# One expert pair moved last and done in half, the exponential table loaded first, and constants taken off ScalarE's queue

## The chip, the cores and the metric

The kernel runs on one core of a Trainium2 chip. The metric is the device time of one execution in microseconds (us). It was taken three times on the chip, and one further execution was profiled.

## What is computed

Three layers run one after the other; only the last one's rows leave the chip.

```python
x = attention(q, k, v)            # 4 x 8 heads x 576 x 64; half the heads local, half strided by 32
x = x / rms(x) * rms_g            # 2304 rows of 512
x = (silu(x @ w_gate) * (x @ w_val)) @ w_out          # d_ff 1536
logits = x @ w_gate2 + modality_bias[modality_id]     # 8 experts
e_idx = argmax(logits); gate_w = softmax(logits)[e_idx]
for e in range(8):                # each row goes through one expert only
    h = relu(x[e_idx == e] @ w1[e])                   # 512 -> 1024
    out[e_idx == e] = gate_w * (h @ w2[e])            # 1024 -> 512
```

Computed with the reference's own inputs, 103, 403, 237, 255, 427, 442, 192 and 245 rows go to experts 0 to 7. Of the first 2048 rows these are 96, 367, 223, 224, 372, 377, 173 and 216.

## The kernel before

The work is split into stretches that a scheduler lays out engine by engine, except the last one, which is written out by hand (`tc.manual_schedule()`).

**Front.** Attention is cut into units (a part of a batch's heads each). A unit's `scores` puts matrix products into a bank of the accumulator memory, VectorE masks them (L202), ScalarE takes the exponential (L212), VectorE divides by the sum, TensorE transposes (L241), ScalarE copies (L243), TensorE multiplies by v (L252), ScalarE copies out (L261, L267). `fill` (L120) issues matmuls on a tile of ones that nobody reads: 40 ahead of all, and 10 ahead of each of the first twelve units' scores. Loads of q, k and v go over SyncE's queue; constants and the gate weights (`raw`, L440, 36 pieces of 512 KB) go over ScalarE's queue. A piece of `raw` is converted in three steps: `conv_a` on GpSimd (L446), `conv_b` on VectorE (L450), `conv_c` on ScalarE and VectorE (L457, L458). Loads share eight completion semaphores in turn, and a load waits until the load that had its semaphore last has landed.

**Chunks.** The rows go in 9 chunks of 256 through the gated layer: `gate_val` (L505 to L507), `gelu_post` (L513 to L519), `ff_out` (L530 to L532). Each product of two 32-bit numbers is three matmuls on parts h and l. `slot()` places the remaining attention and conversions between; `at(s, f)` hangs a function on slot s. Chunks 0 and 1 are interleaved. Each chunk's rows are routed (`route_t` to `route_i`) and written to memory (`rows_d`).

**Experts.** An expert's rows are cut into pairs of two blocks of 128. `first_tables` (L861 on) sorts the experts when 2048 rows are routed: the one with most rows first, and the others in cyclic order behind it; it gives SyncE the first expert's number (`mi`, L869), and SyncE loads its weights (`stg`, L872). `tables` orders the pairs. The program has a fixed part for `BASE = 11` pairs; more pairs than that run under two `tc.If`, at the end. For a pair, `gather` picks row numbers on VectorE and fetches rows by an indirect load on GpSimd's queue (L982), `x_transpose` turns them (L1010) and splits them (L1014, L1015), `mm1` (L1032 to L1034) makes 96 matmuls of 256 columns, `relu_split` (L1042, L1043) the hidden layer, `mm2` (L1056 to L1058) 48 matmuls of 512 columns, and `finish` scales and writes rows by an indirect store (L1072). `split` (L998, L999) makes the next expert's weights into h and l. The last of the fixed pairs does `mm2` block by block, so that the first block's `finish` lies beside the second block's matmuls.

Of the kernel before, what the change touches and what calls it, by code (L numbers as in the profile page):

```python
# [10 lines left out]
F32 = mybir.dt.float32  # L11
# [15 lines left out]
CH = 256  # L27
# [21 lines left out]
def moe_kernel(  # L49
# [72 lines left out]
    n_fill = [0]  # L122

# [45 lines left out]
    def attention(u, banks):  # L169
# [7 lines left out]
        def scores():  # L177
# [5 lines left out]
            if n_fill[0] < 12:  # L183
                n_fill[0] += 1
                fill(sps[:, 384:], 10)
# [507 lines left out]
    tri32 = tmp_p.tile([128, 128], F32, tag="tmp", name="tri32")  # L693
# [4 lines left out]
    A.dma_start(out=wg_sb, in_=w_gate)  # L698
    mb = const.tile([128, 2, E], F32, name="mb")
    A.dma_start(out=mb, in_=mbias.unsqueeze(0).to_broadcast([128, 2, E]))  # L700
    md = const.tile([128, NT, 2], I32, name="md")
    A.dma_start(out=md, in_=modal.bitcast(I32).rearrange("p (t w) -> p t w", w=2))
    mf = tmp_p.tile([128, NT, 2], F32, tag="tmp", name="mf")
    V.tensor_copy(mf[:, :, 1], md[:, :, 0])
    V.tensor_scalar(out=mf[:, :, 0], in0=mf[:, :, 1], scalar1=-1.0, scalar2=1.0, op0=ALU.mult, op1=ALU.add)
    V.memset(carry, 0.0)
    V.memset(ids, 0.0)
    bt = tmp_p.tile([128, NT, E], F32, tag="tmp", name="bt")
    for m, dst in ((0, bsel), (1, bt)):
        V.tensor_tensor(  # L710
            out=dst,
            in0=mf[:, :, m].unsqueeze(2).to_broadcast([128, NT, E]),
            in1=mb[:, m].unsqueeze(1).to_broadcast([128, NT, E]),
            op=ALU.mult,
        )
    V.tensor_tensor(out=bsel, in0=bsel, in1=bt, op=ALU.add)
# [17 lines left out]
    fill(bank("mx")[:, :128], 40)  # L734
# [55 lines left out]

    DELAY = 2
# [36 lines left out]
    def late_open():  # L828
# [15 lines left out]
        tile_([128, E], "e_l")  # L844
        tile_([128, E, E], "lt")
# [13 lines left out]
        tile_([128, 1], "cnt", I32)  # L859
        tile_([128, 1], "cf")  # L860

    def first_tables():
# [14 lines left out]
        V.tensor_scalar(out=key, in0=iota8, scalar1=mf, scalar2=8.0, op0=ALU.is_lt, op1=ALU.mult)  # L877
# [50 lines left out]
    def tables2():  # L928
# [15 lines left out]
        yield  # L944
        V.tensor_copy(lt["cnt"], lt["cf"])
        yield

    def expert_part(e, i):
        return ew[ds(e, 1), i].rearrange("e p c -> (e p) c")

# [344 lines left out]
```

## Time and profile before

| what | us |
| --- | --- |
| median of three executions (lowest, highest) | 865.37 (864.83, 865.46) |
| the profiled execution, own time | 867.22 |
| its span from first to last instruction | 865.4 |
| TensorE busy in the span | 843.9 |
| VectorE busy | 508.9 |
| ScalarE busy | 381.5 |

The profiled execution took 1.85 us longer than the median run; its span lies 1.8 us below its own time. PE is TensorE's matmuls, PEld its weight loads, DVE VectorE, ACT ScalarE, POOL GpSimd, SP SyncE; a q behind a name is that engine's queue of instructions. Busy shares are averages over stretches with different limits, and a busy PE is not PE at its peak.

### The profile page before, as it was taken

To read this page: it belongs to the slowest core of one execution; us is meant where nothing else is said; L and a number is where in the kernel's file an instruction comes from. 1 tells how busy PE (TensorE), PEld (TensorE's weight loads), DVE (VectorE), ACT (ScalarE), POOL (GpSimd) and SP (SyncE) were. 2 spreads that over 40 slices of the span, in tenths; PEclk is the share of its full clock that TensorE was granted. 3 is DMA by queue.
4 is the path that set the end of the run, shared out by engine and by line. 5 is a ranking of instruction groups with operands and counts; after the bars stand their busy time and mean duration, and the time that the engine had idled before them with its cause. 6 is when DMAs were issued, how large, how long until landed. Compare 5 with 4: busy or idle time off the path is not lost.

```text
span 865.4 us, 18024 instructions
## 1 busy us (share of the span) xinstructions
PE 843.9 (98%) x6872; PEld 763.8 (88%) x6872; DVE 508.9 (59%) x1614; ACT 381.5 (44%) x935; POOL 85.7 (10%) x87
## 2 busy tenths in 40 slices
PE   8799999999999999999999999999999999999995
PEld 7688989998988998999999999998899999999994
DVE  4979984544653553644534536356877666666650
ACT  4756564344453254442332222234554554545440
POOL 1314410000000000000000000001131111111100
PEclk9879999999999999999999999999999999999998
DMA  8959211011111111200000000042396734675000
GB/s 247 355 174 348 93 33 47 19 51 41 47 50 34 38 48 54 54 21 26 6 5 26 1 25 2 2 166 79 105 347 207 226 111 130 227 221 166 25 25 22
DMA packets 33015, 84.46 MB, mean 98 GB/s; under 512 B 5122, under 2 KB 12850, under 8 KB 32920
## 3 DMA queue, kind: packets, MB, share of 16 engines
q1 hardware_dynamic: 23064, 54.50, 19.8%
q10 hardware_dynamic: 6336, 19.26, 6.1%
q0 software_dynamic: 3520, 9.45, 3.2%
q8 instruction: 58, 0.95, 0.5%
q14 instruction: 37, 0.30, 0.1%
HBM read 91.57 MB, written 10.49 MB: 118 GB/s over the span
## 4 chain that ended last, share of the span: by engine, by line
PE 76%; issue 11%; DVE 7%; DMA 3%; ACT 1%; POOL 1%; ACTq 0%; POOLq 0%; DVEq 0%; SPq 0%
PE gv L505 11%; PE gv L506 11%; PE gv L507 10%; PE o L530 5%; PE o L531 5%; PE o L532 5%; PE o L1056 3%; PE o L1058 3%; PE o L1057 3%; PE mx L252 2%; PE s L1032 2%; DVE wf L458 2%; PE s L1033 2%; PE s L1034 2%; PE gv L1032 2%
## 5 line engine op out<-in xcount | busy, mean ns | idle before, releaser
L505 PE MATMUL gv<-xh,wf 128*128 128x256 f32 x864 | 247.1, 287 | 2.4 <-DVE t L515 1.4
L506 PE MATMUL gv<-xl,wf 128*128 128x256 f32 x864 | 245.8, 285 | 0.1
L507 PE MATMUL gv<-xh,wf 128*128 128x256 f32 x864 | 245.8, 285 | 0.0
L505 PEld LDWEIGHTS gv<-xh,wf 128*128 128x128 f32 x864 | 163.5, 190 | 9.6 <-DVE t L515 3.2
L506 PEld LDWEIGHTS gv<-xl,wf 128*128 128x128 f32 x864 | 163.7, 189 | 4.9 <-issue 0.6
L507 PEld LDWEIGHTS gv<-xh,wf 128*128 128x128 f32 x864 | 163.9, 190 | 0.8 <-issue 0.2
L999 DVE TENSOR_TENSOR l<-stg,h 128x1024 fp32r<-128x1024 f32 x88 | 107.1, 1223 | 38.0 <-ACT h L998 37.8
L998 ACT CAST h<-stg 128x1024 fp32r<-128x1024 f32 x88 | 91.6, 1048 | 35.3 <-PE o L1058 25.9
L514 DVE SCALAR_TENSOR_TENSOR t<-t,gv 128x256 f32<-128x256 f32 x108 | 45.0, 417 | 92.0 <-ACT t L513 91.2
L513 ACT ACTIVATE t<-gv 128x256 f32<-128x256 f32 x108 | 41.2, 382 | 124.5 <-PE gv L507 114.5
L518 ACT CAST hh<-t 128x256 fp32r<-128x256 f32 x108 | 43.8, 405 | 79.9 <-DVE t L515 34.8
L530 PE MATMUL o<-wf,hh 128*128 128x512 f32 x192 | 77.0, 401 | 0.0
L531 PE MATMUL o<-wf,hh 128*128 128x512 f32 x192 | 76.1, 396 | 0.0
L532 PE MATMUL o<-wf,hl 128*128 128x512 f32 x192 | 75.0, 397 | 0.0
L1056 PE MATMUL o<-h,hT 128*128 128x512 f32 x176 | 70.6, 401 | 0.0
L1058 PE MATMUL o<-h,hT 128*128 128x512 f32 x176 | 68.8, 391 | 0.0
L1057 PE MATMUL o<-l,hT 128*128 128x512 f32 x176 | 68.5, 389 | 0.0
L519 DVE TENSOR_TENSOR hl<-t,hh 128x256 fp32r<-128x256 f32 x108 | 47.1, 436 | 35.9 <-ACT hh L518 35.5
L212 ACT ACTIVATE pr<-pr,mx 128x54 f32<-128x54 f32 (+1 forms) x160 | 52.4, 348 | 12.5 <-DVE mx L202 12.3
L982 POOL DMA_INDIRECT xg<-rows_d,gi x22 | 24.3, 1104 | 303.1 <-DMA stg<-in 142.8
L1032 PE MATMUL s<-xh,h 128*128 128x256 f32 x176 | 49.7, 282 | 0.0
L1033 PE MATMUL s<-xl,h 128*128 128x256 f32 x176 | 49.5, 281 | 0.0
(212 smaller groups left out, 1552.6 us busy)
## 6 DMA issues: line engine op xcount, KB each, us to landing
stg<-in SPq DMA_DIRECT2D x96, 512.0 KB
raw<-in ACTq DMA_DIRECT2D x36, 511.8 KB
rows_d<-x SPq DMA_DIRECT2D x18, 256.5 KB
qk<-in SPq DMA_DIRECT2D x14, 221.0 KB
qk<-in SPq DMA_DIRECT2D x8, 272.0 KB
qk<-in SPq DMA_DIRECT2D x8, 208.0 KB
v<-in SPq DMA_DIRECT2D x14, 108.0 KB
qk<-in SPq DMA_DIRECT2D x7, 167.0 KB
```

The source lines that it names most:

```text
L505: T.matmul(dst, wh[:, ks], xh[k], start=(k == order[0]), stop=False)
L506: T.matmul(dst, wh[:, ks], xl[k], start=False, stop=False)
L507: T.matmul(dst, wl[:, ks], xh[k], start=False, stop=(k == order[3]))
L530: T.matmul(o, h[:, ms], wh, start=(f == 0), stop=False)
L531: T.matmul(o, h[:, ms], wl, start=False, stop=False)
L532: T.matmul(o, l[:, ms], wh, start=False, stop=(f == NF - 1))
L998: A.copy(h, lt["stg", i])
L999: V.tensor_tensor(out=l, in0=lt["stg", i], in1=h.bitcast(F32), op=ALU.subtract)
L1032: T.matmul(dst, w[0][:, k, cs_], xh, start=(k == 0), stop=False)
L1056: T.matmul(ys[t][m], hh, w[0][:, c], start=(q == 0 and c == 0), stop=False)
L1057: T.matmul(ys[t][m], hh, w[1][:, c], start=False, stop=False)
L1058: T.matmul(ys[t][m], hl, w[0][:, c], start=False, stop=(q == 3 and c == 1))
```

## The change

Three things are edited. (1) `first_tables` looks for experts whose number of blocks is odd (estimated from the first 2048 rows), puts the last-numbered of them at the end of the order, and the eleventh pair runs through a new function `half_pair`, for its first block alone. Its second block, and the pairs past eleven, stand under a new `tc.If`. (2) The exponential's table load stands at ScalarE's start, in front of an exponential of an unread tile. Five loads (`tri32`, `iota`, `wg_sb`, `mb`, `md`) go from ScalarE's queue to GpSimd's, and what VectorE makes of them stands at slot 40. (3) `fill` makes 24 matmuls first instead of 40, and none ahead of the first unit.

```diff
-            if n_fill[0] < 12:
-                n_fill[0] += 1
+            if 0 < u < 12:
                 fill(sps[:, 384:], 10)
...
+    warm = sm.tile([128, 4], F32, tag="mx", name="warm")
+    V.memset(warm, 0.0)
...
+    A.activation(out=warm, in_=warm, func=AF.Exp)
...
-    A.dma_start(out=tri32, in_=cst3[:, 5])
-    V.tensor_copy(tri, tri32)
-    A.dma_start(out=iota, in_=iot)
...
-    fill(bank("mx")[:, :128], 40)
+    fill(bank("mx")[:, :128], 24)
...
+    def routing_constants():
+        tri32 = tmp_p.tile([128, 128], F32, tag="tmp", name="tri32")
+        G.dma_start(out=tri32, in_=cst3[:, 5])
+        V.tensor_copy(tri, tri32)
+        G.dma_start(out=iota, in_=iot)
+        G.dma_start(out=wg_sb, in_=w_gate)
...
+    at(40, routing_constants)
...
+        V.tensor_scalar(out=lt["ti"], in0=carry, scalar1=NCH / (NCH - 1.0), scalar2=127.0, op0=ALU.mult, op1=ALU.add)
...
+        V.tensor_reduce(out=hi, in_=od, op=ALU.max, axis=AX.X)
...
-                x_transpose(t + 1, s - 4)
+                x_transpose(t + 1, s - 4, (0,) if t + 2 == BASE else (0, 1))
...
+    def half_pair(t, m):
+
+        rs = slice(128 * m, 128 * m + 128)
+        rl = {}
+
+        def first(q):
+            p = bank(("s0", "s1", "gv", "gv")[q], 2 if q > 1 else 1)[:, :CH]
+            w = [a.rearrange("p (k f) -> p k f", k=4) for a in ws[q]]
+            for k in range(4):
+                xh, xl = (a[:, k % 2, rs] for a in xT[t, k // 2])
+                T.matmul(p, xh, w[0][:, k], start=(k == 0), stop=False)
+                T.matmul(p, xl, w[0][:, k], start=False, stop=False)
+                T.matmul(p, xh, w[1][:, k], start=False, stop=(k == 3))
+            r = rl[q] = sl_p.tile([128, CH], F32, tag="t", name="rl")
+            A.activation(out=r, in_=p, func=AF.Relu)
+
+        def turn(q):
+            pt = bank(("pt", "mx")[q % 2])[:, :CH]
+            r = rl.pop(q)
+            for c in range(2):
+                T.transpose(pt[:, c * 128:c * 128 + 128], r[:, c * 128:c * 128 + 128], ident)
...
+            A.copy(h, pt)
+            V.tensor_tensor(out=l, in0=pt, in1=h.bitcast(F32), op=ALU.subtract)
+
+        def second(q):
+            y = ys[t][m]
+            w = [a.rearrange("p (c d) -> p c d", c=2) for a in ws[4 + q]]
+            for c in range(2):
+                hh, hl = (hT[q][:, i, c * 128:c * 128 + 128] for i in range(2))
+                T.matmul(y, hh, w[0][:, c], start=(q == 0 and c == 0), stop=False)
+                T.matmul(y, hh, w[1][:, c], start=False, stop=False)
+                T.matmul(y, hl, w[0][:, c], start=False, stop=(q == 3 and c == 1))
+
+        ys[t] = {m: bank(f"o{m}")}
+        first(0)
+        first(1)
+        turn(0)
+        first(2)
+        turn(1)
+        first(3)
+        turn(2)
+        second(0)
+        turn(3)
+        for q in (1, 2, 3):
+            second(q)
+        finish(t, (m,), True)
...
+            if t == BASE - 1:
+                half_pair(t, 0)
+                return
...
+        left = nc.values_load(lt["more"][0:1, 0:1], min_val=0, max_val=N + NP2)
+        with tc.If(left > 0):
...
+            with tc.If(second > 0):
+                for q in range(2):
+                    x_transpose(BASE - 1, q, (1,))
+                half_pair(BASE - 1, 1)
```

The start of ScalarE's order before: eight loads of constants stand ahead of the table load and the first eleven exponentials (`pr`), and the first weight piece (`raw`) behind these.

```order
1 L691 DMA cs<-in 128x256
2 L692 DMA cs<-in 128x128
3 L694 DMA tri_128<-in 128x128
4 L696 DMA iota<-in 128x161
5 L697 DMA g_sb<-in 128x4
6 L698 DMA wg_sb<-in 128x32
7 L700 DMA mb<-in 128x16
8 L702 DMA md<-in 128x36
9 L212 ACT_TABLE_LOAD
10 L212 ACTIVATE pr<-pr,mx 128x54 x11
11 L440 DMA raw<-in 128x2047
```

The same place with the change.

```order
1 L692 DMA cs<-in 128x256
2 L681 ACT_TABLE_LOAD
3 L681 ACTIVATE warm<-warm 128x4
4 L693 DMA cs<-in 128x128
5 L694 DMA g_sb<-in 128x4
6 L209 ACTIVATE pr<-pr,mx 128x54 x11
7 L437 DMA raw<-in 128x2047
8 L240 COPY ptS<-o_256 54x512
9 L209 ACTIVATE pr<-pr,mx 128x54 x2
10 L240 COPY ptS<-pt 54x512
11 L209 ACTIVATE pr<-pr,mx 128x54 x2
12 L437 DMA raw<-in 128x2047
```

The table load now stands behind one load, and two loads are left between it and the exponentials. The second `raw` load stands one copy later than before; in the built program it takes the semaphore of an early load of v, where before it took that of the first `raw` load. The third `raw` load now waits for the first.

The start of GpSimd's order with the change; before, the 36 conversions (`CAST top<-raw`) followed the memset without anything between.

```order
6 L679 MEMSET top 128x1024
7 L775 DMA iota<-in 128x161
8 L776 DMA wg_sb<-in 128x32
9 L778 DMA mb<-in 128x16
10 L780 DMA md<-in 128x36
11 L443 CAST top<-raw 128x512 x14
12 L773 DMA tri_1892<-in 128x128
13 L443 CAST top<-raw 128x512 x22
```

Four loads come ahead of the first conversion, and the load of `tri` between the 14th and the 15th. VectorE's conversion of `tri` stands, with the change, in front of a `conv_b` (`raw<-raw,top`) behind the four maskings of a unit that before began at 73.23 us.

VectorE's order in `first_tables` with the change, from the maximum over the experts' counts (`carry`) to the number that SyncE waits for (`mi`); `ti` and `od` are new.

```order
1256 L872 TENSOR_REDUCE m<-carry 128x1
1257 L886 TENSOR_SCALAR ti<-carry 128x8
1258 L631 TENSOR_TENSOR rw<-rw,oh 128x16
1259 L873 TENSOR_SCALAR key<-carry,m 128x8
1260 L887 TENSOR_SCALAR ti<-ti 128x8
1261 L636 TENSOR_REDUCE sc<-rw 128x4
1262 L874 TENSOR_TENSOR key<-key,iota 128x8
1263 L890 CAST od<-ti 128x8
1264 L516 TENSOR_TENSOR hl<-t,hh 128x256
1267 L891 SCALAR_TENSOR_TENSOR od<-iota,od 128x8
1268 L642 TENSOR_SCALAR si<-si 128x2
1269 L876 TENSOR_SCALAR mi<-m 128x1
```

Four new instructions stand ahead of `mi`; six more stand behind it.

## Rows read from the trace of the kernel before

**Rows 1.** The page: busy us, share of the span and instructions of each engine.

```profile
PE 843.9 (98%) x6872; PEld 763.8 (88%) x6872; DVE 508.9 (59%) x1614; ACT 381.5 (44%) x935; POOL 85.7 (10%) x87
```

**Rows 2.** Four stretches: length, busy us of PE, PEld, DVE, ACT, POOL, clock, DMA.

```profile
0.00:18.00 18.00, 15.25 (x229) 13.21 (x229) 6.70 (x60) 5.91 (x19) 1.90 (x6) 1.00 0.83 230
18.00:49.00 31.00, 24.02 (x314) 19.03 (x314) 27.22 (x113) 22.74 (x63) 8.00 (x10) 0.74 0.80 296
49.00:116.00 67.00, 65.73 (x570) 59.45 (x570) 63.42 (x181) 40.40 (x124) 25.09 (x26) 0.97 0.56 199
...
597.00:856.00 259.00, 259.00 (x1705) 235.19 (x1703) 164.37 (x258) 123.84 (x160) 45.59 (x41) 1.00 0.46 151
```

**Rows 3.** Timeline, TensorE about the last pair and a transpose of rows.

```profile
778.01 0.60 PE L1010 MATMUL pt<-cs,xg 128*128 128x128 f32 x4
778.37 0.47 PE L1056 MATMUL o<-h,hT 128*128 128x512 f32 x1
...
833.58 0.28 PE L1032 MATMUL s<-xh,h 128*128 128x256 f32 x1
833.70 0.28 PE L1033 MATMUL s<-xl,h 128*128 128x256 f32 x1
...
855.43 0.39 PE L1057 MATMUL o<-l,hT 128*128 128x512 f32 x1
855.66 0.39 PE L1058 MATMUL o<-h,hT 128*128 128x512 f32 x1
```

**Rows 4.** Timeline, ScalarE's and VectorE's share of a pair, and the end.

```profile
836.63 0.60 ACT L1042 ACTIVATE hT<-s 128x512 fp32r<-128x512 f32 x1 [1.21 <-PE s L1034]
837.26 0.69 DVE L1043 SCALAR_TENSOR_TENSOR hT<-s,hT 128x512 fp32r<-128x512 f32 x1 [0.52 <-ACT hT L1042]
...
857.64 0.98 POOL L1072 DMA_INDIRECT out<-y,gi  x1 [4.49 <-ACT y L1067]
```

**Rows 5.** DMA issues of GpSimd: count, median us from issue to landing.

```profile
xg<-rows_d,gi POOLq DMA_INDIRECT x22, 3.5
out<-y,gi POOLq DMA_INDIRECT x22, 4.8
```

**Rows 6.** Timeline of the first 18 us: warm-up, table load, first weight pieces.

```profile
1.06 5.05 PEld L120 LDWEIGHTS <-ones 128*128 128x128 bf16 x50 [1.06 <-DVE ones L682]
6.22 0.67 PE L191 MATMUL s<-qk 64*64 64x54 f32 x16
6.82 0.56 PEld L120 LDWEIGHTS <-ones 128*128 128x128 bf16 x10
6.88 1.28 ACT L212 ACT_TABLE_LOAD   x1 [6.88 <-DMA g_sb<-in]
9.89 0.36 ACTq L440 DMA_DIRECT2D raw<-in  x1
17.53 0.53 ACT L267 COPY xs<-mx 128x216 f32<-128x216 f32 x1 [3.58 <-DMA raw<-in]
18.05 0.69 DVE L450 SCALAR_TENSOR_TENSOR raw<-raw,top 128x512 int32<-128x512 int32 x1 [3.69 <-POOL top L446]
21.17 0.76 POOL L446 CAST top<-raw 128x512 f16<-128x512 bf16 x1 [3.15 <-DMA raw<-in]
48.84 0.80 PE L505 MATMUL gv<-xh,wf 128*128 128x256 f32 x2 [0.73 <-ACT xh L410]
```

**Rows 7.** Timeline about the first pair's rows: the expert's number, the gather, TensorE's wait.

```profile
573.33 0.15 DVE L869 TENSOR_SCALAR mi<-m 128x1 int32<-128x1 f32 x1
...
594.46 0.55 PE L1010 MATMUL pt<-cs,xg 128*128 128x128 f32 x3 [0.34 <-DMA xg<-rows_d,gi]
```

**Rows 8.** Timeline: VectorE's work on constants before, GpSimd's conversions, an indirect load's issue.

```profile
10.50 0.30 DVE L710 TENSOR_TENSOR bsel<-mf,mb 128x144 f32<-128x144 f32 x1
...
70.33 2.10 POOL L446 CAST top<-raw 128x512 f16<-128x512 bf16 x2 [2.48 <-DMA raw<-in]
...
627.15 1.97 POOL L982 DMA_INDIRECT xg<-rows_d,gi  x1 [0.30 <-DVE l L999]
```

More of the change, by code (lines that the diff above doesn't have):

```diff
@@ L120, in fill @@
             T.matmul(dst, ones16, ones16, start=True, stop=True)
-    n_fill = [0]
     def geometry(u):
@@ L844, in late_open @@
         tile_([128, E], "e_l")
+        tile_([128, E], "od")
         tile_([128, E, E], "lt")
@@ L859, in late_open @@
         tile_([128, 1], "cnt", I32)
+        tile_([128, 2], "more", I32)
         tile_([128, 1], "cf")
@@ L886, in first_tables @@
         V.scalar_tensor_tensor(out=lt["base"], in0=col_e, scalar=0.5, in1=top, op0=ALU.mult, op1=ALU.add)
-        V.tensor_scalar(out=last, in0=mf, scalar1=1.0, scalar2=8.0, op0=ALU.is_lt, op1=ALU.mult)
-        V.scalar_tensor_tensor(out=last, in0=mf, scalar=-1.0, in1=last, op0=ALU.add, op1=ALU.add)
+        V.tensor_scalar(out=last, in0=hi, scalar1=1.0, scalar2=8.0, op0=ALU.is_lt, op1=ALU.mult)
+        V.scalar_tensor_tensor(out=last, in0=hi, scalar=-1.0, in1=last, op0=ALU.add, op1=ALU.add)
         V.tensor_scalar(out=lt["e_l"], in0=iota8, scalar1=last, scalar2=None, op0=ALU.subtract)
@@ L946, in tables2 @@
         yield
+        V.tensor_scalar(out=lt["cf"], in0=lt["cf"], scalar1=1.0 - BASE, scalar2=0.0, op0=ALU.add, op1=ALU.max)
+        yield
     def expert_part(e, i):
@@ L989, in gather, with more @@
             )
+    def more():
+        V.tensor_copy(lt["more"][:, 1:2], lt["pz0"][:, 0, 1:2])
+        V.tensor_tensor(out=lt["more"][:, 0:1], in0=lt["pz0"][:, 0, 1:2], in1=lt["cf"], op=ALU.add)
     ws = {}
@@ L1001, in moe_kernel, with x_transpose @@
     xT = {}
-    def x_transpose(t, q):
+    def x_transpose(t, q, blocks=(0, 1)):
         xg = lt[f"xg{t % 2}"]
@@ L1096, in step @@
         load(ef, s)
+    def half_pair(t, m):
[16 more added lines that the diff above has]
+                T.transpose(pt[:, c * 128:c * 128 + 128], r[:, c * 128:c * 128 + 128], ident)
+            if q not in hT:
+                hT[q] = wts.tile([128, 2, 512], F32R, tag=f"w{24 + q}", name="hT")
+            h, l = (hT[q][:, i, :CH] for i in range(2))
+            A.copy(h, pt)
[21 more added lines that the diff above has]
+        finish(t, (m,), True)
+        ys.pop(t, None)
     def run(t0, t1, first=False):
@@ L1112, in run @@
                 gather(t + 2)
+                if t + 3 == BASE:
+                    more()
             if t - 1 in ys:
@@ L1187, in moe_kernel @@
         run(1, BASE)
-        ni = nc.values_load(lt["cnt"][0:1, 0:1], min_val=0, max_val=NP2)
-        with tc.If(ni > BASE - 1):
-            run(BASE, BASE + 2, True)
-        with tc.If(ni > BASE + 1):
-            run(BASE + 2, NP2, True)
+        left = nc.values_load(lt["more"][0:1, 0:1], min_val=0, max_val=N + NP2)
+        with tc.If(left > 0):
+            second = nc.values_load(lt["more"][0:1, 1:2], min_val=0, max_val=N)
+            ni = nc.values_load(lt["cnt"][0:1, 0:1], min_val=0, max_val=NP2)
+            with tc.If(second > 0):
+                for q in range(2):
+                    x_transpose(BASE - 1, q, (1,))
+                half_pair(BASE - 1, 1)
+            with tc.If(ni > BASE - 1):
+                run(BASE, BASE + 2, True)
+            with tc.If(ni > BASE + 1):
+                run(BASE + 2, NP2, True)
 def _constants():
```

56 lines of the change are left out of this document (31 added, 25 removed).

## The prediction

> **What bounds the kernel now.** I read the page first, for the engine that is busy nearly throughout: TensorE, at 98% of the span, where VectorE has 59% and ScalarE 44% [rows 1]. An average hides stages, so I then cut the span into stretches [rows 2]. The reader is to see three kinds. From 597 to 856 us, in the expert pairs, TensorE is busy for all of 259.00 us: whatever is taken from its work there comes off the end. From 49 to 116 us it is busy for 65.73 of 67, while VectorE, which still converts gate weights, has 63.42: TensorE sets the pace, with VectorE close behind. Before 49 us TensorE's work bounds nothing: it is busy 24.02 of 31 us from 18 on, most of that on fragments and matmuls that nobody reads, while VectorE has 27.22 and DMA a share of 0.80 to 0.83. The end of that stretch is the first gate matmul, at 48.84 [rows 6]. From there the program is one long TensorE stream, so the kernel's time is the time of that first matmul, plus the stream, plus a tail. Each part of the change acts on one of these three.
>
> **A: the last pair in half.** The ordering formula scales the counts at 2048 rows by 9/8: 96 becomes 108, one block, and expert 0 alone has an odd number. At the end it holds 103 rows, so its second block is empty and eleven pairs suffice. The last pair before runs from 833.58 to 856.05 (855.66 plus 0.39), 22.47 us [rows 3]. Its matmuls start every 0.12 us (833.58 to 833.70) at 256 columns and every 0.23 us at 512 (855.43 to 855.66). The half pair has 48 of the first sort, the same shape with operands exchanged, 5.76 us; 24 of the second, 5.52; and 8 transposes, where four took 0.36 (778.01 to 778.37), 0.72. With the last matmul's own end past its successor's place, 0.16, that is 12.16. So 10.3 us go, and half of the eight transposes of the pair's rows in the pair ahead, 0.36: 10.7 in all.
>
> What could lie open is the new way from one product to the next: relu on ScalarE, turn on TensorE, copy on ScalarE, subtraction on VectorE. Twice the width takes 0.60 on ScalarE and 0.69 on VectorE [rows 4]. Between a `first` and its `turn` stands another `first` of 1.4 us, and between the last `turn` and the `second` that reads it two `second`s of 2.8 us, so each is covered. Without cover, at most four turns by some 0.6 would come back, 2.4. Bounds: 8.3 to 10.7; I take 10.7, since the cover is twice what it hides. Expert 0's weights load and split beside the pair ahead, as any new expert's do.
>
> **B: the tail.** Before, engines jump over two conditional bodies in turn; now over one. No row shows a jump. The last store is issued at 857.64 [rows 4] and a store lands 4.8 after that [rows 5], at 862.4; the span ends at 865.4. These 3.0 us hold two jumps and the closing; one jump is a third of them, 1.0. Bounds 0 and 3.0, since a longer jump can also cost what the other saves.
>
> **C: the front.** (1) 50 warm-up weight loads took 5.05 us ahead of the first scores at 6.22, 0.101 each; the next ten 0.56, 0.056 each [rows 6]. So TensorE began at the lower of its two levels, 1.2 GHz, although the granted-clock column prints 1.00 for the stretch [rows 2]. 26 fewer are worth 2.6 us at that pace; the first scores, of which 16 took 0.67 at the higher level, now run at the lower one and give back some 0.7. (2) The table load began at 6.88, behind eight loads' issue, with the first exponentials behind it at 8.2 [rows 6]. It now starts near 1.2 and is over by 2.5: off the path. (3) Both bring the first weight piece, issued at 9.89, forward by about a microsecond. Everything stops for its landing: ScalarE waits 3.58 us up to 17.53 because the second piece's issue waits for the first's semaphore, and VectorE 3.69 up to 18.05. DMA's share was 0.83 in that stretch, so the same bytes cannot land much earlier: I take 1.2. (4) The second piece no longer waits for the first, so GpSimd's next wait of 3.15 (at 21.17) shortens, and of VectorE's 3.8 idle us between 18 and 49 (31.00 less 27.22) I take 1.5. Together 2.7. Bounds: nothing, if DMA holds the first piece where it is; and 6.2, if the start's 2.5 and VectorE's whole 3.69 both go.
>
> **D: ten more small VectorE instructions in `first_tables`.** Four stand ahead of `mi`, each at most 0.15 [rows 7]. On `mi` hang SyncE's weight loads, then VectorE's splits, behind which the first gather's row numbers stand; and TensorE already waited 0.34 for those rows at 594.46. So this delay is not covered: 0 to 0.6 lost, I take 0.4. The two new steps for `more` and the later six fall into VectorE's idle time, 95 us in the pairs [rows 2].
>
> **E: constants on GpSimd's queue.** Four loads go out while GpSimd would idle, far ahead of 17 us. `tri` stands behind the 14th conversion; the 15th waited 2.48 us for a weight piece before 70.33 [rows 8], which hides an issue of up to 1.97 (the slowest row of an indirect load). Issued at 67.9 and landing in 3.5 [rows 5], it is there at 71.4, ahead of VectorE's reading near 74. VectorE gains six instructions of up to 0.30 [rows 8], 1.8 us, in a stretch where it idles 3.6 of 67: bounds 0 to 1.8, I take 0.3.
>
> Here a rule speaks against the change. The row shows indirect issues of up to 1.97 us beside a busy VectorE, against a landing time of 3.5. The Trainium skill (SBUF — State Buffer, "A bandwidth-pool intuition that's wrong") says that a load issued by GpSimd may be held up while VectorE holds the port that the two share, and gives a load of 0.62 us that took 3.1. By that fivefold the `tri` load would land an estimate of 17 us after its issue, some 11 behind its reader, and the sum would be an estimate of 863 if all of that passed on; the trace shows no such factor, and the fourth rival below takes the mechanism with a price from rows.
>
> **Sum.** −10.7 −1.0 −2.7 +0.4 +0.3 = −13.7. Against the profiled execution's own 867.22 that is 853.5; against the median, which is 1.85 less, **851.7 us**.
>
> **The rivals.**
> 1. *The front gives nothing*: the first piece lands when DMA has moved all that stands ahead of it (share 0.83 [rows 2]), whoever asked earlier. Against it: the second piece's freed semaphore. 851.7 + 2.7 = 854.4. Chance 0.20.
> 2. *The front gives its bound*, 6.2: VectorE's wait of 3.69 disappears altogether. 848.2. Chance 0.14.
> 3. *The clock stays low.* With fewer warm-ups, TensorE does not reach 2.4 GHz near 6 us. A weight load then takes 0.101 in place of 0.056 [rows 6]; the 15.25 us of TensorE work in the first 18 us [rows 2], of which some 9 lie behind 6.2 us, would take 1.8 times as long: 7 us more, of which the 2.75 us that it idles cover a part. The front is 4.5 late rather than 2.7 early: 858.9. For it: the clock shares of 0.74 and 0.97 show that it does fall [rows 2]. Against: the second unit's ten fillers can follow the first scores at once. The Trainium skill (TensorE: Matmul & The Clock Gate, "What's actually happening") says that the throttled state is the default and that activity releases it; the trace agrees, 0.101 against 0.056. Chance 0.10.
> 4. *A load on GpSimd's queue comes late*, and VectorE and the conversions stand behind it: `tri` one conversion wait more (2.48 [rows 8]). 854.2. If longer, TensorE's lead in converted weights runs out. Chance 0.08.
> 5. *The last block is not the last.* If more than 128 rows reached the last expert, the new conditional would run the second block: 12.2 us of matmuls, two uncovered transposes with copies (some 2.5), and up to 3.0 of jumps, 17.7 on top: 869.4, slower than before. The count of 103 speaks against it. Chance 0.03.
>
> **How the numbers follow.** The forecast, with its terms near the values taken, has 0.45. Rivals 1 and 4 lie within 3 us of it, rival 2 within 3.5 on the other side. The range has to leave out no more than 2 in 10: 847.5 to 857.5 leaves out rivals 3 and 5 (0.13) and the far ends of B and of rival 2. Faster by over 0.2% (1.7 us, about what a measurement of this kernel can tell from no change) holds in all but rival 5 and worse mixtures of rival 3: 0.95. Within 0.2%: 0.01. Slower: 0.04.
>
> **What would show it.** A: 48 matmuls of the last pair start every 0.12 us and no gap over 0.3 us stands before a turn; the last pair takes 12 us, the one ahead 22.9. B: from last matmul to the end of the span 8.3 us, not 9.3. C: the first exponential near 5 us, the first `conv_b` at 16 to 17, the first gate matmul at 45 to 47. D: TensorE's wait at the first gather's rows 0.6 to 0.9. E: no wait of VectorE for `tri`. The forecast is wrong above all if the first gate matmul's 2.7 us are lost again between 49 and 173 us, where VectorE has little left to give, or if the scheduler's new order puts a wait of its own there.

## The result and the profile after

Three executions of the changed kernel took 852.07, 852.62 and 854.47 us (a fourth took 1337.18 at a mean granted clock of 0.556 and is left out); the kernel before took 864.83 to 866.50 in four beside them. The ratio is 0.9855, with a 95% interval of 0.9832 to 0.9877: 12.5 us less, 10.6 to 14.5. The forecast was 851.7, in a range of 847.5 to 857.5. The profiled execution took 852.62, its span 850.8.

The page of the changed kernel, in the order of [rows 1]: TensorE has lost 13.7 us of work, VectorE none.

```profile
PE 830.2 (98%) x6778; PEld 750.3 (88%) x6778; DVE 509.0 (60%) x1625; ACT 380.4 (45%) x939; POOL 87.6 (10%) x91
```

Its first three stretches, as in [rows 2]. DMA has gone from 0.83 to 0.89 in the first; VectorE from 63.42 to 64.54 in the third.

```profile
0.00:18.00 18.00, 15.69 (x247) 13.25 (x247) 8.04 (x67) 8.84 (x27) 4.22 (x10) 1.00 0.89 248
18.00:49.00 31.00, 23.10 (x280) 18.53 (x281) 26.61 (x112) 22.25 (x68) 7.90 (x9) 0.75 0.81 291
49.00:116.00 67.00, 65.37 (x597) 58.94 (x597) 64.54 (x181) 39.15 (x114) 25.82 (x27) 0.99 0.55 196
```

**The half pair.** TensorE's timeline at the start of the pair ahead (L1057), about the first turn (L1143), and at the end:

```profile
808.49 0.28 PE L1057 MATMUL s<-xh,h 128*128 128x256 f32 x1
...
831.36 0.28 PE L1133 MATMUL s<-h,xh 128*128 128x256 f32 x1
831.48 0.28 PE L1134 MATMUL s<-h,xl 128*128 128x256 f32 x1
...
834.24 0.38 PE L1143 MATMUL pt<-cs,rl 128*128 128x128 f32 x2
834.37 0.36 PE L1133 MATMUL gv<-h,xh 128*128 128x256 f32 x1
...
843.24 0.39 PE L1157 MATMUL o<-h,hT 128*128 128x512 f32 x1
```

The stretch from 831.36 to 843.63 by itself, in the order of [rows 2]: its length, then TensorE's busy time.

```profile
831.36:843.63 12.27, 12.27 (x81) 10.90 (x79) 3.59 (x6) 4.22 (x10) 1.97 (x2) 1.00 0.11 44
```

The pitch is 0.12 us (831.36 to 831.48), the last pair takes 12.27 (12.16 worked out), and TensorE is busy for all of it. The pair ahead takes 22.87 (808.49 to 831.36); in the kernel before it took 23.24, from the row below to 833.58 [rows 3].

```profile
810.34 0.28 PE L1032 MATMUL s<-xh,h 128*128 128x256 f32 x1
```

ScalarE's and VectorE's rows show why no turn waits:

```profile
833.10 0.37 ACT L1137 ACTIVATE rl<-s 128x256 f32<-128x256 f32 x1
...
834.72 0.37 ACT L1147 CAST hT<-pt 128x256 fp32r<-128x256 f32 x1
```

```profile
835.11 0.43 DVE L1148 TENSOR_TENSOR hT<-pt,hT 128x256 fp32r<-128x256 f32 x1 [0.58 <-ACT hT L1147]
```

The relu is over at 833.47 and its turn is due at 834.24, behind the second `first`. The first `hT` is whole at 835.54, 2.1 us ahead of the first `second` (837.68).

**The tail.** The last store of the changed kernel, to compare with the last line of [rows 4]:

```profile
845.17 0.98 POOL L1097 DMA_INDIRECT out<-y,gi  x1 [7.86 <-ACT y L1092]
```

From there to the end of the span (850.8) pass 5.63 us, where it was 7.76 (857.64 to 865.4).

**The front.** Three engines' timelines of the changed kernel, to compare with [rows 6]: warm-ups; table load, first exponentials and the first two weight pieces; the first conversion; the first gate matmul.

```profile
1.10 2.74 PE L120 MATMUL mx<-ones 128*128 128x128 bf16 x24 [1.10 <-DVE ones L683]
3.63 0.95 PE L120 MATMUL s<-ones 128*128 128x128 bf16 x7
```

```profile
1.19 1.28 ACT L681 ACT_TABLE_LOAD   x1 [1.19 <-PEq L1370]
...
5.93 1.03 ACT L209 ACTIVATE pr<-pr,mx 128x54 f32<-128x54 f32 x4 [3.24 <-DVE mx L199]
...
8.69 0.34 ACTq L437 DMA_DIRECT2D raw<-in  x1
...
12.12 0.33 ACTq L437 DMA_DIRECT2D raw<-in  x1
```

```profile
16.30 0.69 DVE L447 SCALAR_TENSOR_TENSOR raw<-raw,top 128x512 int32<-128x512 int32 x1 [2.02 <-POOL top L443]
```

```profile
46.30 0.58 PE L502 MATMUL gv<-xh,wf 128*128 128x256 f32 x1 [0.73 <-ACT xh L407]
```

The second piece goes out at 12.12 (17.15 before), VectorE's wait is 2.02 (3.69), and the first gate matmul stands at 46.30 (48.84): 2.54 earlier, where 2.7 were forecast.

**The other terms.** GpSimd's load of `tri`, VectorE's use of it without a wait, and TensorE's wait at the first gathered rows ([rows 7] has 0.34):

```profile
65.03 0.54 POOL L773 DMA_DIRECT2D tri<-in  x1
```

```profile
71.40 0.21 DVE L774 CAST tri<-tri 128x128 bf16<-128x128 f32 x1
```

```profile
592.48 0.55 PE L1036 MATMUL pt<-cs,xg 128*128 128x128 f32 x3 [0.22 <-DMA xg<-rows_d,gi]
```

### The profile page after: what moved, and what is told of

Read it like the earlier page. It is cut to its first block, busy times and chain, and to the rows that moved or that the text cites. A ratio compares the mean times of both kernels' runs of the same rounds, so it can differ in the third digit from the quotient of the medians.

```text
span 850.8 us, 17842 instructions
## 1 busy us (share of the span) xinstructions
PE 830.2 (98%) x6778; PEld 750.3 (88%) x6778; DVE 509.0 (60%) x1625; ACT 380.4 (45%) x939; POOL 87.6 (10%) x91
## 5 line engine op out<-in xcount | busy, mean ns | idle before, releaser
L502 PE MATMUL gv<-xh,wf 128*128 128x256 f32 x864 | 246.9, 287 | 2.1 <-DVE t L512 1.3
L502 PEld LDWEIGHTS gv<-xh,wf 128*128 128x128 f32 x864 | 163.4, 190 | 9.4 <-DVE t L512 3.0
L1081 PE MATMUL o<-h,hT 128*128 128x512 f32 x160 | 64.4, 402 | 0.0
L1083 PE MATMUL o<-h,hT 128*128 128x512 f32 x160 | 62.6, 391 | 0.0
L1082 PE MATMUL o<-l,hT 128*128 128x512 f32 x160 | 62.3, 389 | 0.0
L512 DVE TENSOR_TENSOR t<-t,gv 128x256 f32<-128x256 f32 x108 | 45.0, 417 | 1.9
L1057 PE MATMUL s<-xh,h 128*128 128x256 f32 x160 | 45.2, 282 | 0.0
```

What stands on the lines that cost most here:

```text
L502: T.matmul(dst, wh[:, ks], xh[k], start=(k == order[0]), stop=False)
L1057: T.matmul(dst, w[0][:, k, cs_], xh, start=(k == 0), stop=False)
L1081: T.matmul(ys[t][m], hh, w[0][:, c], start=(q == 0 and c == 0), stop=False)
L1082: T.matmul(ys[t][m], hh, w[1][:, c], start=False, stop=False)
L1083: T.matmul(ys[t][m], hl, w[0][:, c], start=False, stop=(q == 3 and c == 1))
```

## The experiments

For each kernel, TensorE's timeline gives three places: the first gate matmul, the first one of chunk 2 (behind the interleaved chunks 0 and 1), and the start of the last one on `xh` (L505 before, L502 after). In the changed kernel the latter two are:

```profile
171.85 0.28 PE L502 MATMUL gv<-xh,wf 128*128 128x256 f32 x1
...
590.60 0.28 PE L502 MATMUL gv<-xh,wf 128*128 128x256 f32 x1
```

| kernel | median us | ratio to before (95%) | first gate | chunk 2 | last gate | last gate to end |
| --- | --- | --- | --- | --- | --- | --- |
| before | 865.4 to 866.4 | 1 | 48.84 | 172.79 | 592.46 | 272.9 |
| changed | 852.6 | 0.9855 (0.9832, 0.9877) | 46.30 | 171.85 | 590.60 | 260.2 |
| 1 half alone | 855.25 | 0.9864 (0.9837, 0.9891) | 50.92 | 174.57 | 594.47 | 260.0 |
| 2 front alone | 864.75 | 0.9977 (0.9961, 0.9993) | 46.58 | 173.13 | 591.70 | 272.7 |
| 3 constants early | 854.06 | 0.9856 (0.9830, 0.9881) | 47.55 | 171.77 | 590.78 | 259.9 |
| 4 warm-ups back | 859.15 | 0.9922 (0.9896, 0.9948) | 49.72 | 176.72 | 595.49 | 260.8 |
| 5 nested conditionals | 864.56 | 0.9969 (0.9951, 0.9987) | 48.33 | 172.15 | 592.20 | 270.8 |
| 6 second block runs | 871.38 | 1.0043 (1.0025, 1.0061) | 48.14 | 173.88 | 592.85 | 277.0 |
| 7 table at first use | 853.51 | 0.9840 (0.9818, 0.9862) | 47.00 | 173.14 | 591.79 | 259.9 |
| 8 one warm-up | 866.43 | 0.9999 (0.9983, 1.0014) | 59.54 | 186.35 | 605.35 | 260.4 |
| 9 the same, loads first | 862.51 | 0.9949 (0.9930, 0.9967) | 55.44 | 181.23 | 600.03 | 260.2 |
| 10 warm-ups 32 | 854.15 | 0.9858 (0.9831, 0.9885) | 47.56 | 173.78 | 592.29 | 260.2 |
| 11 warm-ups 16 | 858.18 | 0.9897 (0.9869, 0.9925) | 49.35 | 177.38 | 595.61 | 260.5 |
| 12 first piece early | 855.94 | 0.9871 (0.9845, 0.9896) | 48.44 | 174.76 | 593.88 | 260.6 |

The last column is the span's end less the last gate matmul: it holds the pairs and the tail. In every kernel with the half pair, its second block not run, it is 259.9 to 260.8.

**1. The half alone.** The front's code and order are those of before.

```diff
+            if t == BASE - 1:
+                half_pair(t, 0)
+                return
...
+        with tc.If(left > 0):
```

> The kernel before with the first edit alone: the pair with the odd block last, run as a half, and everything past it under one outer conditional. The front is that of before. My theory: the half pair and its tail carry nearly all of the gain, and the front adds what is left. After minus before is 865.4 - 852.6 = 12.8 us in the fast runs; the last pair gave 10.7 by the traces, the tail from the last output row to the end 2.2 (9.3 to 7.1), less up to 0.4 for the new steps on VectorE. So 853.0 to 853.8, with the first gate matmul at 48.8 as before. By the terms as predicted (10.7, 1.0, 0.4) 854.1. Rival, the front gives nothing that lasts: this kernel alone reaches the changed one's 852.6. Rival, half and front need each other (the tail's 2.2 is not the half pair's): 855 or more.

Measured: 0.9864, 11.8 us less (9.4 to 14.1); the median lies 10.5 below, less than my 12. The end is as expected (260.0 against 272.9), but the first gate matmul stands at 50.92, 2.1 later than in the profile of before, although the order of instructions up to there is the same. TensorE's granted clock in the stretch from 18 to 25 us was 0.50 here, 0.61 in the profile of before and 1.00 in experiment 5, which has that order too and starts its gate matmuls at 48.33. So the front is known from one profile to some 1.3 us only. The half pair carries the gain; the rival that needs no front is not excluded by the times (0.9864 against 0.9855), but experiment 2 speaks against it.

**2. The front alone.**

```diff
-    fill(bank("mx")[:, :128], 40)
+    fill(bank("mx")[:, :128], 24)
...
+    A.activation(out=warm, in_=warm, func=AF.Exp)
...
+    at(40, routing_constants)
```

> The kernel before with the second and third edits alone: the table load first, five loads on GpSimd's queue with VectorE's work on them at slot 40, and 26 warm-up matmuls fewer. All 22 half blocks run as before. My theory: the first gate matmul comes 2.5 us earlier (46.3), about 1.0 of that is lost again at 238 us, where TensorE waits for a bank that ScalarE has to copy first, and 1.5 to 1.8 us arrive at the end: 863.6 to 863.9. By the terms as predicted (2.7 less 0.3) 863.0. Rival, the front gives nothing at the end: 865.4. Rival, the whole 2.5 arrive and the loss at 238 us is made up elsewhere: 862.9.

Measured: 0.9977, 2.0 us less (0.6 to 3.4), by medians 1.0. The first gate matmul stands at 46.58; the end keeps its 272.7. So the front gives something, near what was expected, and it doesn't need the half.

**3. Constants early.** The five loads go out on GpSimd's queue at the program's start.

```diff
+    routing_constants()
...
-    at(40, routing_constants)
```

> The changed kernel with the five constants' loads and VectorE's work on them issued at the start of the program, still on GpSimd's queue, and not at slot 40. In this order the transposes of the row scale (chunk 3's) stand among the products of the chunk before again, as in the kernel before, and no longer straight ahead of the attention outputs that want the same bank. My theory: the slot-40 placement moved them there, and the wait of 0.99 us behind ScalarE's copy at 239 us goes: 1.0 us faster than the changed kernel, about 851.6, and no wait over 0.3 us of TensorE for that copy. Rival, the wait only moves or VectorE's work comes back as a delay of the front: the changed kernel's 852.6, or up to 0.5 more, since VectorE waits 2.0 us for weights at 16 us and has room for 1 us of small work.

Measured: 0.9856, the changed kernel's ratio. A miss: the transposes did return to their old place, and nothing was won. The wait that was to go is this one, of the changed kernel:

```profile
239.64 0.61 PE L249 MATMUL mx<-ptS,v 54*64 54x54 f32 x13 [0.99 <-ACT r L394]
```

From chunk 2 to the last gate matmul this kernel takes 419.0 us and the changed kernel 418.75. The changed kernel's order has ten matmuls more ahead of chunk 2 and ten fewer behind it (the counts stand under C below), and it reaches chunk 2 at the same time (171.85 and 171.77): what it does earlier makes up for the wait. A stall in a different order is not a loss until the stretch is summed.

**4. Warm-ups back.**

```diff
-    fill(bank("mx")[:, :128], 24)
+    fill(bank("mx")[:, :128], 40)
...
-            if 0 < u < 12:
+            if n_fill[0] < 12:
+                n_fill[0] += 1
```

> The changed kernel with the 16 and 10 warm-up matmuls put back (40 first, and 10 ahead of the first unit). Table load and constants stay as in the changed kernel. My theory: in the changed kernel the first scores stand at 4.52 us behind 31 weight loads of 0.104; 26 more by 0.06 to 0.104 put them at 6.1 to 6.2 as before, the first conversion on VectorE and the first gate matmul come some 0.5 to 1.5 us later, and the time is 853.1 to 854.1. Rival, the warm-ups cost nothing, since the first weight piece's landing sets the front: 852.6. Rival, warm-ups gave a higher clock and the changed kernel lost by having fewer: 852.0 or less.

Measured: 0.9922, 6.5 us over the changed kernel by medians and 5.8 by the ratios, far more than 26 weight loads cost. Its first gate matmul is 3.4 later, and chunks 0 and 1 take 127.0 us against 125.55. TensorE's waits between 49 and 83 us (line, what it waited for, total, times, longest), of this kernel:

```profile
PE gv L505 <- ACT xh L410: 2.7, 2, 1.8
PE mx L241 <- ACT xs L267: 1.0, 1, 1.0
PE gv L506 <- DVE xl L411: 0.4, 1, 0.4
```

and of the changed kernel:

```profile
PE mx L249 <- ACT ptS L240: 0.2, 1, 0.2
```

Of the first line's 2.7 us, 1.84 stand ahead of the first gate matmul, where the changed kernel has 0.73; they belong to the 3.4, and so do 16 matmuls of a unit's scores that this order has ahead of it. The other waits, 2.3 us, lie in chunks 0 and 1. All but 0.4 us are on ScalarE's copies, and the scheduler's order is another one here. A kernel with all the warm-ups and none of the other front edits (experiment 1) is faster than this one: the front's edits don't add up.

**5. Nested conditionals.** Before, with one jump in place of two.

```diff
         with tc.If(ni > BASE - 1):
             run(BASE, BASE + 2, True)
-        with tc.If(ni > BASE + 1):
-            run(BASE + 2, NP2, True)
+            with tc.If(ni > BASE + 1):
+                run(BASE + 2, NP2, True)
```

> The kernel before with one thing changed: the second of its two conditionals at the end stands inside the first, so that engines jump once over both bodies and not twice. Nothing else moves. It prices the tail alone. In the kernel before 7.76 us pass from the last store's issue (857.64) to the end of the span (865.4); in the changed kernel 5.63 (845.17 to 850.8). My theory now: the whole of these 2.1 us is the second jump, so the last store to the end takes 5.6 here too, and the time is 863.6 against 865.7. By the price in the prediction (1.0 for a jump): 6.8, and 864.7. Rival, the shorter tail comes from the half pair (less in flight when the last store goes out): 7.8, and 865.7.

Measured: 0.9969, 2.7 us less (1.1 to 4.2), by medians 1.8. Its last store, then that of experiment 1:

```profile
857.31 0.98 POOL L1072 DMA_INDIRECT out<-y,gi  x1 [4.49 <-ACT y L1067]
```

```profile
849.08 0.99 POOL L1092 DMA_INDIRECT out<-y,gi  x1 [7.85 <-ACT y L1087]
```

From the store to the end pass 5.69 us (to 863.0) without any half pair, and 5.42 (to 854.5) with one; two jumps had 7.76. So the second jump is worth 2.1, and the half pair's part in it is at most the 0.3 by which these two differ.

**6. The second block runs.**

```diff
-        V.tensor_copy(lt["more"][:, 1:2], lt["pz0"][:, 0, 1:2])
-        V.tensor_tensor(out=lt["more"][:, 0:1], in0=lt["pz0"][:, 0, 1:2], in1=lt["cf"], op=ALU.add)
+        V.tensor_scalar(out=lt["more"][:, 1:2], in0=lt["pz0"][:, 0, 1:2], scalar1=1.0, scalar2=None, op0=ALU.add)
+        V.tensor_scalar(out=lt["more"][:, 0:1], in0=lt["cf"], scalar1=1.0, scalar2=None, op0=ALU.add)
```

> The changed kernel with 1 added to both numbers that the conditionals look at, so that the outer conditional and the second block of the last pair do run; that block's row numbers are out of bounds here and its stores write nothing. It prices the fifth rival of the prediction: 17.7 on top (12.2 of matmuls, 2.5 of transposes and copies without cover, up to 3.0 of jumps), 853.6 + 17.7 = 871.3, slower than the kernel before. My theory: between 14.7, without the jumps, and 17.7. Rival, the body of the conditional has to wait on something that the profile has not shown so far (its code, its store after the first block's): over 20 on top, 874 or more.

Measured: 871.38 us, 1.0043, slower than before. The last gate matmul to the end takes 277.0, 16.8 more than in the changed kernel. TensorE's first matmul of the second block, and GpSimd's two last stores:

```profile
848.66 0.39 PE L1133 MATMUL s<-h,xh 128*128 128x256 f32 x1 [2.33 <-ACT xh L1040]
```

```profile
847.43 0.98 POOL L1097 DMA_INDIRECT out<-y,gi  x1 [7.86 <-ACT y L1092]
862.95 0.98 POOL L1097 DMA_INDIRECT out<-y,gi  x1 [14.54 <-DVEq L1279]
```

The stores lie 15.5 us apart, and the last has 6.85 to the end where the changed kernel has 5.63: 16.7 in all, with the 2.33 that TensorE waits for uncovered copies.

**7. The table at its first use.**

```diff
-    A.activation(out=warm, in_=warm, func=AF.Exp)
```

> The changed kernel without the unread exponential at the start, so that the table load stands at its first use again. Only three loads stand ahead of it on ScalarE's queue now, where the kernel before had eight. My theory: with five loads gone ScalarE is through with its issues at about 2.1 us, loads the table from then to 3.4, and the first scores are there only at 4.52 to 5.6; the exponentials start near 5.9 as in the changed kernel, and the time is the changed kernel's, 852.6 to 854. Taking the loads off the queue was the edit that counted. Rival, the table load waits with its exponential for the first masked scores, and 1.28 us come back at the front: first exponentials at 7.2, and 853.9 to 855.3.

Measured: 0.9840, not slower than the changed kernel. ScalarE's rows of this kernel:

```profile
2.16 1.28 ACT L209 ACT_TABLE_LOAD   x1 [2.16 <-issue]
5.73 1.03 ACT L209 ACTIVATE pr<-pr,mx 128x54 f32<-128x54 f32 x4 [2.28 <-DVE mx L199]
```

The table load doesn't wait with its exponential, and the exponentials start at 5.73 (5.93 in the changed kernel). So loading the table first gained nothing that can be measured. The exponentials start 2.2 us earlier than before (5.93 against 8.2) for two other reasons: in experiment 4, with five loads off ScalarE's queue but all 50 warm-ups, they start at 7.24, and the rest comes with the 26 warm-ups that the changed kernel leaves out.

**8. One warm-up.**

```diff
-    fill(bank("mx")[:, :128], 24)
+    fill(bank("mx")[:, :128], 1)
```

> The changed kernel with one warm-up matmul at the start in place of 24 (the ten ahead of each unit from the second on stay). It asks what the rest of the warm-ups are worth. The first scores would stand at 4.4 us or a little earlier, when q and k have landed, against 4.52. My theory: the clock rises within the next units' fillers anyway, somewhat later (16 score matmuls took 1.10 us at the start in the changed kernel, 0.67 at the higher clock), and the front comes out within 1 us of the changed kernel's: 852.6 to 854. Rival (the third of the prediction), TensorE stays at the lower of its levels well into the front: first gate matmul at 49 or later, 856 or more. Second rival, the order that the scheduler makes out of fewer instructions is what counts, as in the run with the warm-ups put back, where ScalarE's copies stood in another order and TensorE waited 3.7 us for them: then the time can go either way by more than 2 us, with the same clock.

Measured: 0.9999. The whole gain is gone, and all of it in the front: the first gate matmul stands at 59.54. TensorE's timeline of this kernel shows the lower level for two units and part of the third (1.11 us for 16 products; 0.67 at the higher, [rows 6]):

```profile
3.83 1.11 PE L188 MATMUL s<-qk 64*64 64x54 f32 x16 [1.38 <-DMA qk<-in]
5.68 1.11 PE L188 MATMUL s<-qk 64*64 64x54 f32 x16 [0.74 <-DMA qk<-in]
...
7.89 0.89 PE L188 MATMUL s<-qk 64*64 64x54 f32 x12
```

Behind that the weight pieces come late: ScalarE's timeline has a conversion that waits, and only then the third load (15.40 in the changed kernel).

```profile
17.97 0.65 ACT L454 CAST wf<-raw 128x512 fp32r<-128x512 f32 x1 [3.93 <-DVE raw L447]
...
19.91 0.33 ACTq L437 DMA_DIRECT2D raw<-in  x1
```

The stretches of this kernel from 18 to 40 us (last columns: granted clock, DMA's share, GB/s),

```profile
18.00:25.00 7.00, 3.44 (x42) 2.67 (x44) 4.73 (x24) 4.67 (x13) 1.92 (x2) 0.70 0.73 246
...
32.00:40.00 8.00, 5.32 (x62) 4.50 (x61) 7.44 (x26) 4.90 (x13) 2.89 (x3) 0.79 0.53 193
```

and of the changed kernel, where DMA is busy throughout:

```profile
18.00:25.00 7.00, 5.68 (x97) 4.64 (x97) 4.78 (x28) 4.64 (x15) 1.70 (x2) 1.00 1.03 333
25.00:32.00 7.00, 5.73 (x77) 4.52 (x72) 7.00 (x27) 5.67 (x17) 3.74 (x4) 0.76 1.03 398
32.00:40.00 8.00, 4.13 (x50) 3.23 (x50) 8.00 (x28) 5.89 (x17) 2.46 (x3) 0.81 1.02 391
```

**9. One warm-up, loads first.** ScalarE's conversions stand behind as many loads as in the changed kernel.

```diff
+        with tc.issue_after(ld_op[min(LOADS[n], len(ld_op) - 1)].ins) if n < 8 else ExitStack():
-        A.copy(w[:, 0], wk)
+            A.copy(w[:, 0], wk)
```

> The kernel with one warm-up matmul again (866.4 us, first gate matmul at 59.5), with one thing fixed: on ScalarE's queue the loads of the weight pieces stand as many ahead of the conversions as in the changed kernel (five ahead of the first conversion, eight ahead of the second, and so on). In the run with one warm-up only two loads stood ahead of the first conversion; ScalarE waited 3.9 us in that conversion, the third load went out at 19.9 us (15.4 in the changed kernel), and DMA's share fell to 0.73, 0.60 and 0.53 between 18 and 40 us, where the changed kernel has 1.02. My theory: it is this order, chosen by the scheduler, that lost 13 us, and not the clock. With the loads first, DMA's share from 18 to 40 is 0.95 or more, the first gate matmul stands at 46 to 50, and the time is 853 to 857. Rival, the lower clock of the first 12 us does it: the order changes little, 862 or more, with the first gate matmul at 55 or later.

Measured: 862.51, first gate matmul at 55.44. The numbers are the rival's. But the condition of my theory wasn't met either: with the conversion out of the way the third load still goes out only at 18.88, behind an exponential that waits 2.92 us for VectorE, and DMA's share from 18 to 40 is 0.87, 0.81 and 0.66.

```profile
18.00:25.00 7.00, 2.83 (x51) 2.31 (x52) 4.75 (x25) 3.65 (x11) 2.29 (x3) 0.77 0.87 289
...
32.00:40.00 8.00, 5.63 (x67) 4.60 (x65) 6.71 (x26) 5.20 (x15) 2.02 (x3) 0.79 0.66 192
```

The order of loads and conversions explains 3.9 of the 13 us (866.4 to 862.5). The rest is the lower clock, or the order of everything else that changed with the count; these runs don't tell them apart.

**10 and 11. 32 and 16 warm-ups.**

```diff
-    fill(bank("mx")[:, :128], 24)
+    fill(bank("mx")[:, :128], 32)
```

> The changed kernel with 32 warm-up matmuls first in place of 24, none ahead of the first unit. The order of ScalarE's loads, exponentials, copies and conversions in the front stays as in the changed kernel, so this gives the warm-ups' own price. My theory: 8 weight loads of 0.104 us or less put the first scores at 4.9 to 5.3 (4.52 before); the weight pieces' landing covers most of it, and the time is the changed kernel's, 852.6 to 854.2, or up to 0.8 more. Rival, every warm-up is paid for in full and more, as putting back all 26 seemed to say (859.2, some 0.25 us for each): 854.6 to 856.

> The changed kernel with 16 warm-up matmuls first in place of 24. The weight loads keep nearly the changed kernel's place on ScalarE's queue (five ahead of the first conversion); other instructions of the front change places. My theory: fewer warm-ups are worth nothing by themselves, since q and k land only at about 4.3 us and the weight pieces set the rest; 852.6 to 855, the upper end where the other order costs something. Rival, the first scores gain 0.8 us and it arrives: 851.8. Second rival, the clock rises late and the front pays for it: 856 or more.

Measured: 32 give 0.9858, the changed kernel's ratio; 16 give 0.9897, slower. ScalarE's order with 32 is the changed kernel's in the main, but some copies and exponentials change places. Eight warm-ups more cost nothing that can be measured; the interval (0.9831 to 0.9885) is too wide to exclude the rival's 2 us. With 16, the clock rose as early as in the changed kernel (the second unit's 16 products take 0.67 us at 5.54), yet the first gate matmul stands at 49.35 and chunks 0 and 1 take 128.0. The granted clock is lower afterwards: 0.67 from 18 to 49 us (0.75 in the changed kernel) and 0.93 from 49 to 116 (0.99). So the second rival had the wrong moment, but the clock remains a candidate for the loss. Over the counts 1, 16, 24, 32 and 50 (40 and 10) the medians are 866.4, 858.2, 852.6, 854.2 and 859.2: neither end is good, and these runs give no price of one warm-up that could be added to a sum.

**12. The first piece early.**

```diff
     A.dma_start(out=g_sb, in_=rms_g)
+    load_w(0)
+    n_wl[0] = 1
```

> The changed kernel with the first weight piece's load right behind the constants on ScalarE's queue (issued at about 2.1 us in place of 8.69). In the changed kernel DMA's share is 0.70 from 0 to 6 us and 0.91 from 6 to 12, and 1.02 to 1.06 from there to 40: from 12 us on the front is bound by what DMA can move. My theory: the 2.3 us of DMA that idle ahead of 12 us (6 times 0.30 and 6 times 0.09) can be had in part; the first conversion on VectorE comes 2 to 4 us earlier, the first gate matmul 1 to 2 us earlier (45 to 46), and 0.5 to 1.5 us arrive at the end: 851.3 to 852.6 where the changed kernel has 852.6 to 853.6. Rival, the early piece takes its share from q, k and v, the first scores come 1 us later or more, and nothing is won: 853.5 or more.

Measured: 0.9871, not faster, as the rival had it. VectorE's first conversion of this kernel comes 4.8 us earlier,

```profile
11.53 0.69 DVE L447 SCALAR_TENSOR_TENSOR raw<-raw,top 128x512 int32<-128x512 int32 x1
```

and the first gate matmul 2.1 us later, at 48.44. TensorE waited 1.75 us for the third unit's q and k, the second unit's products ran slower (0.97 us for 16, where the changed kernel has 0.67), and the granted clock from 6 to 12 us was 0.84 (1.00). So an earlier first piece does not bring the front forward by itself; since the edit also held up q and k, the run doesn't say what the landing alone is worth.

## Why the prediction was right, and where it wasn't

The time (852.6 against 851.7, in the range) and the sign came out as forecast, since the largest term was right. Two smaller ones were off by about a microsecond each, in opposite directions; that they cancel, and the time comes within a microsecond, is luck.

**A, the half pair: 10.7 forecast, 10.6 measured.** The last pair went from 22.47 to 12.27 and the pair ahead gave 0.4. The cover was as worked out: TensorE was busy for 12.27 of 12.27 us. Across kernels, those with one jump need 270.8 us from the last gate matmul to the end without the half pair (experiment 5) and 260.0 with it (experiment 1), 10.8 for A and D together.

**B, the tail: 1.0 forecast, 2.1 measured.** The step that failed is "one jump is a third of them". The row it rested on bounded it by 3.0, and the split into thirds was a guess; experiment 5 shows 2.1 by the jump alone. The 3.0 can't have been two such jumps and a closing in a row, so some of it runs beside the store's landing; no row shows which part.

**C, the front: 2.7 forecast; 2.4 at the first gate matmul, and about 1.3 at the end.** Three traces have the order of the kernel before in the front (before, experiments 1 and 5): the first gate matmul at 49.4 in the mean, the last at 593.0. Three have that of the changed kernel (changed, experiments 2 and 6): 47.0 and 591.7. Where the other 1.1 goes, two stretches show, from the first gate matmul to chunk 2 and from there to the last gate matmul; first of the kernel before, then of the changed one:

```profile
48.84:172.79 123.95, 122.17 (x1054) 111.04 (x1055) 95.33 (x293) 66.00 (x201) 25.09 (x26) 0.98 0.36 122
172.79:592.46 419.67, 419.32 (x3550) 382.01 (x3549) 211.90 (x884) 160.57 (x490) 4.16 (x4) 1.00 0.13 39
```

```profile
46.30:171.85 125.55, 123.92 (x1064) 111.91 (x1065) 96.38 (x300) 66.68 (x203) 25.82 (x27) 0.98 0.35 120
171.85:590.60 418.75, 417.44 (x3540) 380.26 (x3539) 213.50 (x891) 159.64 (x489) 4.19 (x4) 1.00 0.13 40
```

The first stretch is longer (125.5 to 126.6 us in the three traces, 123.7 to 124.0 in the old order) because ten matmuls more lie in it, four transposes of rows and six of `ff_out`; behind chunk 2 there are ten fewer. TensorE's idle time there did not grow (1.63 us, 1.78 before). So nothing is lost between 49 and 173 us, where the prediction looked for the danger. The loss lies behind chunk 2: TensorE is idle for 1.3 to 1.7 us there, where the old order has 0.35 to 0.8, and 0.99 of it is the wait at 239 us (experiment 3). The prediction feared a wait that the scheduler's new order makes, looked for it elsewhere, and gave it no term.

Of the steps behind the 2.7, these did not hold. (1) and (2): no run gives 26 warm-ups or the table load a price of its own (experiments 10, 11 and 7). (3) "Everything stops for its landing" is not borne out for the first weight piece (experiment 12). (4) GpSimd's wait for the second piece did not shorten (4.18 us up to 20.45, where it was 3.15), and of the 1.5 us that VectorE's idle time from 18 to 49 us was to lose nothing can be told (4.39 us, where it was 3.78; in three traces of the old order 3.8 to 6.3, of the new one 3.8 to 4.8). What did change is the flow of pieces: the second is issued 5 us earlier, and DMA's share from 12 to 18 and from 18 to 25 us is 1.06 and 1.03 (0.95 and 0.96 before). From 32 to 40 VectorE has no idle time (8.00 of 8, as before). TensorE's own account up to the first gate matmul is this: in the mean of the three traces it is busy for 2.6 us less and idle for 0.3 more than in the old order. The 2.4 us are thus about what step (1) gave the removed warm-ups before its deduction, and TensorE waits no less than before; but what caused them was not measured, since putting warm-ups back moved other work as well (experiments 4 and 10).

**D: 0.4 forecast, nothing measured.** TensorE's wait at the first gathered rows is 0.22, not 0.6 to 0.9, and 10.8 for A and D leaves no loss that these traces can tell (the last column differs by up to 0.9 among kernels with the same end).

**E: 0.3 forecast, within the noise.** VectorE never waits for `tri`, its busy time from 49 to 116 us grew by 1.1, and with that work elsewhere the time is the same (experiment 3). By the Trainium skill (SBUF — State Buffer, "A bandwidth-pool intuition that's wrong") a load issued by GpSimd could be held up beside a busy VectorE; this trace shows no such delay. DMA issues of the changed kernel (KB, us to landing):

```profile
iota<-in POOLq DMA_DIRECT2D x1, 80.5 KB, 4.8
...
tri<-in POOLq DMA_DIRECT2D x1, 64.0 KB, 5.0
```

`tri` went out amid a VectorE that was busy for 64.54 of 67 us and landed in 5.0; `iota`, with VectorE nearly idle, in 4.8. The fourth rival is out with it.

**The sum as measured.** 10.8 (A, D), 2.1 (B) and 1.3 (C, E) make 14.2, and 867.22 less 14.2 is 853.0, where the profiled execution took 852.62. The 1.3 is rough: the last gate matmul differs by 2.3 us among traces of one order. By repeated times the two halves are 11.8 and 2.0, 13.8 together, in the interval of 10.6 to 14.5.

**The other rivals.** The first (nothing from the front) is out by experiment 2, whose interval ends at 0.6 us, and the second (6.2) by its other end at 3.4. The third (the clock stays low) did not happen with 24 warm-ups. With one, the time rises by some 13 us, where this rival had 7; how much of that is the clock stays open (experiment 9). The fifth was priced at 17.7 on top of the forecast; measured, the end takes 16.8 more, and the kernel is slower than before, as it said (871.38).

## What to carry to other kernels

Where one engine is busy throughout, work taken from it can be summed from its pitch, to a tenth of a microsecond here, once the cover of each new hand-over is checked. Where several engines and DMA share the limit and a scheduler places the work, edits don't add: forecast the net of the stretch with a wide range, measure each edit in its place, and compare several traces of the same order before you believe a microsecond. A wait seen in a new order is a loss only when the whole stretch got longer, and a stretch between two marks got longer only if the same work lies between them: count its instructions first.

## What the runs showed of the hardware

A second conditional at the end of this program, its body not run, costs 2.1 us (7.76 to 5.69 from the last store to the end), where 1.0 had been guessed.

Identical orders of instructions reached the first gate matmul at 48.33, 48.84 and 50.92 us in one case and at 46.30, 46.58 and 48.14 in the other. In the first set the granted clock from 18 to 25 us was 1.00, 0.61 and 0.50, in the order of these times. The Trainium skill (TensorE: Matmul & The Clock Gate, "What's actually happening") says that the same kernel leaves the throttled level at different points in different runs; those three traces agree, since TensorE got through 52, 48 and 66 matmuls of the same order in the first 6 us. The clock alone doesn't explain the spread: the second set has 1.00 from 18 to 25 us three times, and 0.75, 0.68 and 0.73 from 18 to 49, and still differs by 1.8 us in another order than these.

The granted-clock column prints 1.00 for the first 18 us of the changed kernel, while its first 24 warm-ups and the products behind them ran at the lower level's pace: what says so is the duration of equal matmuls (16 products took 1.10 us at 4.52 and 0.67 at 6.29), not the column.
